# Batch 0's queries and keys loaded as rows of four tokens and turned by plain products, with a new order of work

## The chip, the cores and the metric

The kernel runs on one core of a Trainium2 chip. The metric is the device time of one execution in microseconds (us). The kernel before took 963.61 us (median of three runs, 963.43 to 965.06).

## The reference

Attention over 4 batches, 8 heads, 576 tokens and 64 columns a head, in two branches that are added, and then two MLP layers over all 2304 tokens. Cut to what matters:

```python
q_d, k_d, v_d = (t.reshape(B, H, S // 4, 4, D).mean(axis=3) for t in (q, k, v))
out_up = np.repeat(sm_attn(q_d, k_d, v_d), 4, axis=2)        # the pooled branch
mask = np.abs(pos[:, None] - pos[None, :]) < 4               # the local branch
scores = np.where(mask, scale * np.matmul(q, k.transpose(0, 1, 3, 2)), -1e9)
out_local = np.matmul(softmax(scores), v)
x = (out_up + out_local).transpose(0, 2, 1, 3).reshape(B * S, H * D)
h = x @ w_in
x = np.where(h > 0, h, np.exp(np.minimum(h, 0)) - 1) @ w_out
g = x @ w_gate
return (g / (1 + np.exp(-g)) * (x @ w_val)) @ w_o2
```

## The kernel before, in words

**Tokens and chunks.** A batch is cut into `NU` = 6 units of `U` = 96 tokens; three units (`UPC`) make a chunk of 288 tokens, so the first MLP layer runs over `NC` = 8 chunks, two for each batch. In each chunk it takes `NF1` = 16 steps: a step makes 128 hidden columns (`gemm1`, four products over the 512 input columns), applies the nonlinearity on ScalarE and VectorE, and adds their share to the four output banks (`gemm2`). In chunk 0 (`add_whole`, L929) these are plain fp32 products (L940, L945). In chunks 1 to 7 (`add_first`, L960) each operand is split into a high and a low part, and `products` (L911) multiplies three pairs of parts (L915 to L917). Tile `g` holds the high part of the hidden columns and, by a subtraction on GpSimd (L995), the low one. The second MLP layer follows and ends the run; the order in which it runs is touched by the change only through costs and due times.

**Weights.** They arrive as 64-bit words. `add_weights` (L396) loads a block of 512 KB on SyncE (L363, L368), and makes its fp32 words with two passes on ScalarE (L404, L407) and two on VectorE (L411, L413). `add_weights_away` does the same for the second layer's weights in halves, and stores them to DRAM (tiles `mid`, `wd`).

**Attention of batch 0.** `add_unit` (L616) loads 96 query rows and 112 key rows of all eight heads per unit (L494, runs of 256 B), turns each with four transpositions on TensorE (L633) into a tile for that unit, copies it out of PSUM, and sums queries and keys over four tokens (`add_sums`, L512). `add_local` (L529) does the banded scores of a unit (L541), the mask (L558), the maximum (L563), its subtraction, the exponential, the sum (L572), the weighting, a transposition on VectorE (L580), the spreading into the block-diagonal tile `bd`, and the value products (L606) into `f`. `add_pooled` (L685) does the pooled branch for a pair of heads: sums of values (`add_rows`, L696 on VectorE or L700 and L701 on GpSimd), scores (L717), maxima (L724), exponentials (L730), weighting (L740), transpositions (L758), value products (L774) into `xdT`. `add_split` (L885) adds `f` and `xdT` to `x`, the input of the first MLP layer; chunk 0 needs units 0 to 2 and all four head pairs.

**Attention of batches 1 to 3** runs beside the first MLP layer. `add_turned` (L648) loads queries and keys block by block (L662, runs of 128 B) into the tiles `qT` and `kT` of the whole batch, and VectorE transposes each block in place (L667). `add_double` does two units at a time, `add_pooled_all` (L781) the pooled branch.

**What sets the order.** All work is given to a planner (`Work`, L138) as tasks with an engine (or a choice of two), a cost in us, a due time, tiles read and written. `run` plays the engines forward by these costs, starts on each free engine the ready task that is due first, and emits it; so the costs and due times decide the order of each engine's instructions, and nothing else. The program then runs each engine in that order, with semaphores. The due times hang on a few numbers:

```python
START, STEP0, STEP, STEP2 = 48.0, 4.1, 3.45, 7.9
EAGER, URGENT, FREE, SLACK = 15.0, 14.0, 8.0, 1.0
spans = {1: (18, 25), 2: (40, 50), 3: (70, 80)}
```

`time1(s)` is the planned time of step `s`; `spans` says in which steps the attention of a batch is due.

## Time and profile before

| | |
|---|---|
| median of three runs | 963.61 us |
| the profiled execution | 962.43 us |
| its span on the core | 960.6 us |
| first product of the first MLP layer starts at | 49.22 us |
| TensorE matmul busy | 924.7 us (96%) |
| VectorE / ScalarE / GpSimd busy | 587.9 / 519.6 / 488.8 us |
| mean granted TensorE clock | 0.982 |

The busy time of TensorE counts pipelined products and is no measure of how close it is to its peak; what can be read from it is where it stands still. A time in a row counts from the start of the span. A line number is that of the kernel before; the changed kernel's lines are up to some 12 lower.

### The profile page before, as it was taken

To read this page: it belongs to the slowest core of one execution; us is meant where nothing else is said; L and a number is where in the kernel's file an instruction comes from. 1 tells how busy PE (TensorE), PEld (TensorE's weight loads), DVE (VectorE), ACT (ScalarE), POOL (GpSimd) and SP (SyncE) were. 2 spreads that over 40 slices of the span, in tenths; PEclk is the share of its full clock that TensorE was granted. 3 is DMA by queue.
4 is the path that set the end of the run, shared out by engine and by line. 5 is a ranking of instruction groups with operands and counts; after the bars stand their busy time and mean duration, and the time that the engine had idled before them with its cause. 6 is when DMAs were issued, how large, how long until landed. Compare 5 with 4: busy or idle time off the path is not lost.

```text
span 960.6 us, 20374 instructions
## 1 busy us (share of the span) xinstructions
PE 924.7 (96%) x7738; PEld 838.2 (87%) x7738; DVE 587.9 (61%) x1023; ACT 519.6 (54%) x1191; POOL 488.8 (51%) x554
## 2 busy tenths in 40 slices
PE   6799999999989999999899999999999999999998
PEld 4577788899979999999899988888888887899998
DVE  5999777988886687646115567222222225886773
ACT  3878864665744665656445564634333426444441
POOL 5322994564553433428932537998777939100000
PEclk8689999999999999999999999999999999999999
DMA  9899514945673444546432254440313269953331
GB/s 173 251 319 250 93 40 121 164 144 141 162 159 94 129 135 124 154 128 199 149 94 81 83 184 182 162 176 23 121 51 114 99 208 322 314 165 112 124 129 44
DMA packets 189730, 142.07 MB, mean 148 GB/s; under 512 B 101184, under 2 KB 170944, under 8 KB 189632
## 3 DMA queue, kind: packets, MB, share of 16 engines
q1 hardware_dynamic: 189488, 140.50, 50.0%
q8 instruction: 61, 1.00, 0.4%
q14 instruction: 37, 0.30, 0.1%
q10 hardware_dynamic: 144, 0.26, 0.1%
HBM read 96.68 MB, written 44.04 MB: 146 GB/s over the span
## 4 chain that ended last, share of the span: by engine, by line
PE 85%; DVE 5%; ACT 2%; POOL 2%; SPq 2%; DMA 2%; issue 2%; DVEq 0%; ACTq 0%; POOLq 0%
PE bank L915 25%; PE bank L917 24%; PE bank L916 24%; PE bank L940 4%; PE bank L945 3%; PE bank L606 1%; PE bank L541 1%; SPq L662 1%; PE bank L817 1%; PE bank L823 1%; PE warm L1416 0%; DVE e L988 0%; PE bank L870 0%; DMA kT<-in_k_dram 0%; DMA x2d<-o 0%
## 5 line engine op out<-in xcount | busy, mean ns | idle before, releaser
L995 POOL TENSOR_TENSOR g<-e,g 128x288 fp32r<-128x288 f32 x112 | 96.3, 861 | 150.3 <-ACT g L307 115.6
L915 PE MATMUL bank<-x,w 128*128 128x288 f32 x448 | 136.3, 304 | 10.0 <-DVE e L988 9.8
L915 PE MATMUL bank<-g,w 128*128 128x288 f32 x448 | 135.2, 302 | 0.0
L916 PE MATMUL bank<-x,w 128*128 128x288 f32 x448 | 132.9, 297 | 1.6 <-POOL x L903 1.6
L915 PE MATMUL bank<-xs,wu 128*128 128x512 f32 x336 | 132.6, 395 | 0.5 <-DVE blk L1119 0.5
L916 PE MATMUL bank<-g,w 128*128 128x288 f32 x448 | 132.1, 295 | 0.7 <-issue 0.7
L916 PE MATMUL bank<-xs,wu 128*128 128x512 f32 x336 | 132.6, 395 | 0.0
L917 PE MATMUL bank<-xs,wu 128*128 128x512 f32 x336 | 132.6, 394 | 0.0
L917 PE MATMUL bank<-x,w 128*128 128x288 f32 x448 | 132.4, 296 | 0.0
L917 PE MATMUL bank<-g,w 128*128 128x288 f32 x448 | 131.8, 294 | 0.0
L1119 DVE TENSOR_TENSOR blk<-bank,blk 128x512 f32<-128x512 f32 x72 | 49.7, 691 | 99.1 <-PE bank L917 90.7
L915 PE MATMUL bank<-os,ys 128*128 128x256 f32 x378 | 107.3, 284 | 1.5 <-DVE o L1119 1.0
L917 PE MATMUL bank<-os,ys 128*128 128x256 f32 x378 | 107.0, 283 | 0.4 <-DVE ys L1087 0.4
L916 PE MATMUL bank<-os,ys 128*128 128x256 f32 x378 | 106.9, 283 | 0.0
L988 DVE SCALAR_TENSOR_TENSOR e<-e,bank 128x288 f32<-128x288 f32 x112 | 50.1, 449 | 82.9 <-ACT e L992 76.9
L915 PEld LDWEIGHTS bank<-x,w 128*128 128x128 f32 x448 | 84.6, 189 | 14.4 <-DVE e L988 13.1
L1116 ACT COPY blk<-bank 128x512 f32<-128x512 f32 x72 | 42.2, 586 | 88.6 <-PE bank L917 87.2
L984 ACT ACTIVATE e<-bank 128x288 f32<-128x288 f32 x112 | 45.7, 410 | 80.4 <-PE bank L917 50.8
L916 PEld LDWEIGHTS bank<-x,w 128*128 128x128 f32 x448 | 85.2, 190 | 1.9 <-POOL x L903 1.8
L915 PEld LDWEIGHTS bank<-g,w 128*128 128x128 f32 x448 | 84.0, 187 | 3.2 <-issue 1.5
L917 PEld LDWEIGHTS bank<-g,w 128*128 128x128 f32 x448 | 84.5, 189 | 0.8 <-issue 0.8
L917 PEld LDWEIGHTS bank<-x,w 128*128 128x128 f32 x448 | 85.1, 190 | 0.0
(170 smaller groups left out, 2315.2 us busy)
## 6 DMA issues: line engine op xcount, KB each, us to landing
yr<-yd SPq DMA_DIRECT2D x27, 512.0 KB
yd<-blk SPq DMA_DIRECT2D x24, 512.0 KB
os<-od SPq DMA_DIRECT2D x42, 256.0 KB
u<-wd SPq DMA_DIRECT2D x40, 256.0 KB
wd<-mid SPq DMA_DIRECT2D x72, 128.0 KB
w<-in_moe_w_in_dram SPq DMA_DIRECT2D x16, 512.0 KB
w<-in_moe_w_out_dram SPq DMA_DIRECT2D x16, 512.0 KB
w<-in_moe_w_out_dram SPq DMA_DIRECT2D x24, 256.0 KB
```

The source lines that it names most:

```text
L541: nc.tensor.matmul(sc[j].t[s * QB:(s + 1) * QB, (u * NP + p) * QB:(u * NP + p + 1) * QB], q_of(p)[j * D:(j + 1) * D, a:a + QB], k_of(p)[j ...
L606: nc.tensor.matmul(pvs[u].t[j * D:(j + 1) * D, p * U:(p + 1) * U], tvs[u].t[:, (2 * p + j) * D:(2 * p + j + 1) * D], bd.t[:, u, j * NP + p ...
L915: nc.tensor.matmul(ps, sh, mh, start=first, stop=False, skip_group_check=more)
L916: nc.tensor.matmul(ps, sh, ml, start=False, stop=False, skip_group_check=more)
L917: nc.tensor.matmul(ps, sl, mh, start=False, stop=last, skip_group_check=more)
L940: nc.tensor.matmul(h.t[:, :T1], wi.t[:, i * P:(i + 1) * P].bitcast(F32), x.t[:, i, 0].bitcast(F32), start=i == 0, stop=i == NP - 1)
L945: nc.tensor.matmul(acc[0][i].t[:, :T1], wo.t[:, i * P:(i + 1) * P].bitcast(F32), ge(), start=f == 0, stop=f == NF1 - 1)
L984: nc.scalar.activation(e.t, h.t[:, :T1], AF.Relu, scale=-1.0)
L988: nc.vector.scalar_tensor_tensor(out=e.t, in0=e.t, scalar=-1.0, op0=ALU.add, in1=h.t[:, :T1], op1=ALU.max)
L995: add("pool", 0.82, due - URGENT, lambda e=e, g=g: nc.gpsimd.tensor_tensor(out=g.t[:, 1], in0=e.t, in1=g.t[:, 0], op=ALU.subtract), reads= ...
L1116: return add("act", ps_copy, when(m) - 20, lambda: nc.scalar.copy(d(i), ps.t[:, :w]), reads=[ps], writes=of(i))
L1119: return add("dve", ps_sum, when(m) - 20, lambda: nc.vector.tensor_tensor(out=d(i), in0=ps.t[:, :w], in1=d(i), op=ALU.add), reads=[ps], wr ...
```

## The change

Batch 0 is laid out like the other batches: queries and keys in `qT` and `kT` over the whole batch. `add_unit` is replaced by `add_first_batch`. It issues 16 loads (four head pairs, two halves of the batch, queries and keys) in rows of four tokens: 72 rows, for each of two heads 256 numbers in one run of 1 KB. Each load is turned by eight plain products with the identity (four tokens, two heads), which write every fourth column of a PSUM bank, and copied to `qT` or `kT`. Sums over four tokens are taken per load; key sums are for GpSimd alone. The pooled value sums of batch 0 go to GpSimd alone (`VS`). Tiles of batch 0's softmax lie in parts of weight slots, and two raw weight slots fewer are there for the loads of weights (12, not 14). All other edits are costs, due times and the constants above: batch 1's attention is due in steps 4.5 to 10.8 and not 18 to 25, loads ahead of a batch by 31.6 us and not 14, the conversion of the second layer's weights from 3.2 chunks on and not 2, and so on. Some 30 costs in calls of `add` change by a few hundredths to tenths of a us in the same way as the one of `negative` below.

```diff
-    CHANGE = 0.1
+    CHANGE = 0.15
...
-    U0, U1 = 2, 19
+    U0, U1 = 2, 21
...
-    START, STEP0, STEP, STEP2 = 48.0, 4.1, 3.45, 7.9
+    START, STEP0, STEP, STEP2 = 54.0, 4.58, 3.41, 7.9
     order = [(c, f) for c in range(NC) for f in range(NF1)]
+    VS, VC = EITHER[1:], (1.25,)
+    FIRST, VALUES, LATER, POOLED = -40.0, -30.4, 14.3, 20.4
-    EAGER, URGENT, FREE, SLACK = 15.0, 14.0, 8.0, 1.0
+    EAGER, URGENT, FREE, SLACK = 10.7, -0.6, 12.0, 0.0
...
-        add("pe", 0.8 * n, due + 2 - EAGER, scores, reads=reads, writes=[*sc, sm], slack=SLACK, kind="small", after=then)
+        add("pe", 0.8 * n, due + 2 - EAGER, scores, holds=[x for name in parts for x in parts[name]], writes=[*sc, sm],
+            slack=SLACK, kind="small", after=[*made, *then])
...
-    def add_unit(i, due, load_due, rows, late, v_due, first):
-
-        q0 = i * U
-        k0 = min(max(q0 - 8, 0), S - KU)
-        off = PAD + q0 - k0
-        tq, tk, tv = rows
-        add("sp", 0.5, load_due, lambda: load_rows("q", 0, q0, U, tq.t), writes=[tq], nbytes=U * H * D * 4 * 1.9)
-        add("sp", 0.5, load_due + 0.1, lambda: load_rows("k", 0, k0, KU, tk.t), writes=[tk], nbytes=KU * H * D * 4 * 1.9)
-        add("sp", 2.0, v_due, lambda: load_values(0, q0, tv.t), writes=[tv], nbytes=P * H * D * 4 * 3.1)
-        if i == 0:
-            sums[0] = sum_ring.new()
-        qT, kT = place("qT"), place("kT")
-        for which, t, dst, count, start, own in ((0, tq, qT, U, 0, 0), (1, tk, kT, KU, PAD, off)):
-            pt = att_bank()
-
-            def turn(t=t, count=count, pt=pt):
-                for p in range(NP):
-                    nc.tensor.transpose(pt.t[:, p * count:(p + 1) * count], t.t[:count, p * P:(p + 1) * P], ident[:count, :count])
-
-            def keep(engine, dst=dst, count=count, start=start, pt=pt):
-                copy(engine, dst.t[:, :, start:start + count], pt.t[:, :NP * count].rearrange("p (a t) -> p a t", a=NP))
-
-            add("pe", 0.4, first - EAGER, turn, reads=[t], writes=[pt, dst], slack=SLACK, kind="small")
-            add(COPIER, (0.5, 0.55), first + 1, keep, reads=[pt], writes=[dst], second=1)
-            early.append(add_sums(first + 2, lambda dst=dst, own=own: dst.t[:, :, own:own + U].rearrange("p a (g r) -> p a g r", r=R),
-                lambda which=which: sums[0].t[:, which, :, i * GU:(i + 1) * GU], [dst], [sums[0]], (0.56, 1.1)))
-        xfs = add_local(i, 1, due + late, lambda p: qT.t[:, p], lambda p: kT.t[:, p], [qT, kT], off, [tv])
-        early.extend(qT.readers + kT.readers)
-        return xfs[0]
-
-    early, summed = [], {}
+    def add_first_batch(rows, ready):
+
+        sums[0] = sum_ring.new()
+        parts = {name: [longs[name].new(lambda p=p: [p]) for p in range(NP)] for name in ("qT", "kT")}
+        made = {}
+        for k, (p, u, which) in enumerate((p, u, which) for p in range(NP) for u in range(2) for which in range(2)):
+            name, start = (("qT", 0), ("kT", PAD))[which]
+            t, dst, pt = rows[k], parts[name][p], att_bank()
+            cols = slice(start + u * UPC * U, start + (u + 1) * UPC * U)
+            add("sp", 0.5, FIRST + 0.5 * k, lambda t=t, p=p, u=u, name=name: nc.sync.dma_start(
+                out=t.t, in_=rows_of(name[0], 0, u, 2 * p, 2 * p + 2)), writes=[t], nbytes=HALF * 2048 * 1.2)
+
+            def turn(t=t, pt=pt):
+                for r in range(R):
+                    for j in range(2):
+                        nc.tensor.matmul(
+                            pt.t[j * D:(j + 1) * D, :UPC * U].rearrange("c (g r) -> c g r", r=R)[:, :, r],
+                            t.t[:, j, r * D:(r + 1) * D], ident[:HALF, :HALF], start=True, stop=True)
+
+            add("pe", 0.62, FIRST + k - EAGER, turn, reads=[t], writes=[pt, dst], slack=SLACK, kind="small", after=ready[:1])
+            made[which, p, u] = add(COPIER, (0.41, 0.45), FIRST + k + 1, lambda engine, dst=dst, pt=pt, cols=cols: copy(
+                engine, dst.t[:, cols], pt.t[:, :UPC * U]), reads=[pt], writes=[dst], second=1)
+            summed.setdefault((0, p), []).append(add_sums(
+                FIRST + k + 2, lambda dst=dst, cols=cols: dst.t[:, cols].rearrange("p (g r) -> p g r", r=R),
+                lambda which=which, p=p, u=u: sums[0].t[:, which, p, u * HALF:(u + 1) * HALF], [], [sums[0]], (0.45, 0.9)[which:],
+                holds=[dst], after=[made[which, p, u]], engines=EITHER[which:]))
+        return parts, made
+
+    summed = {}
...
-        if b == 1:
-            clear = lambda: [nc.gpsimd.memset(x.t[:, a:z], 0.0) for x in parts["kT"] for a, z in ((0, PAD), (PAD + S, LONG))]
-            after = [*after, *early, add("pool", 1.0, load_due, clear, writes=parts["kT"], after=early)]
...
-            add(EITHER, (1.0, 1.25), due, lambda engine, u=u, t=t: add_rows(u, t.t, engine), reads=[t], writes=[vs])
+            add(VS, VC, due, lambda engine="pool", u=u, t=t: add_rows(u, t.t, engine), reads=[t], writes=[vs])
...
-        if b:
-            add(EITHER, (0.78, 1.3), due + 4.3, weight, reads=[pr, su], writes=[pr])
-        else:
-            add("dve", 0.78, due + 4.3, lambda: weight("dve"), reads=[pr, su], writes=[pr])
+        add(EITHER, (0.78, 1.15), due + 4.3, weight, reads=[pr, su], writes=[pr])
...
-            add("act", 0.45, due - URGENT, negative, reads=[h], writes=[e])
+            add("act", 0.41, due - URGENT, negative, reads=[h], writes=[e])
...
-        rows = [parts(2) for _ in range(NU)]
+        rows = [x for _ in range(2 * NP) for x in parts(2)]
...
-            xfs[n] = add_unit(n, 4.0 * n, -40 + 2 * n, rows=(*rows[n], vals[n]), late=0.0 if n < UPC else 24.0,
-                v_due=-20.0 + n if n < UPC else 30.0 + n, first=0.5 * n - 8.0)
-            if n == 0:
-                load_mask()
+            late = n >= UPC
+            add("sp", 2.0, LATER + n if late else VALUES + n, lambda n=n: load_values(0, n * U, vals[n].t), writes=[vals[n]], nbytes=P * H * D * 4 * 3.1)
+            turned_by = [t for (which, p, u), t in made.items() if u == (late or 0) or (which and (n == UPC - 1 or n == UPC))]
+            xfs[n], = add_local(n, 1, 2.5 * n + 68.6 * late, parts, turned_by, [vals[n]], ready[1:], (), sms[n])
         for p in range(NP):
-            add_pooled(0, p, 16.0 + 0.5 * p, -28 + p, raws=praws[2 * p:2 * p + 2], pr=probs[p])
+            add_pooled(0, p, POOLED + 1.5 * p, -28 + p, raws=praws[2 * p:2 * p + 2], pr=probs[p], prT=turneds[p])
...
-            return time1(2 * NF1) + (time1(6.9 * NF1) - time1(2 * NF1)) * m / (2 * len(w2))
+            return time1(3.2 * NF1) + (time1(6.5 * NF1) - time1(3.2 * NF1)) * m / (2 * len(w2))
...
-        spans = {1: (18, 25), 2: (40, 50), 3: (70, 80)}
+        spans = {1: (4.5, 10.8), 2: (50.5, 52.5), 3: (76.5, 119.4)}
         split = UPC
         for b in range(1, B):
             lo, hi = (time1(s) for s in spans[b])
             after = [words["in", 10 if b == 1 else NF1 - 1]]
-            parts = add_turned(b, lo, lo - 14, after)
-            add_pooled_all(b, lo + 4, lo - 10, 3.0)
+            parts = add_turned(b, lo, lo - 31.6, after)
+            add_pooled_all(b, lo + 2.3, lo - 24.0, 7.3)
             for m in range(NU // 2):
-                due = lo + 6 + (hi - lo) * 2 * m / NU
-                xfs[b * NU + 2 * m], xfs[b * NU + 2 * m + 1] = add_double(b, m, due, due - 18, parts, after, [words["out", 10]])
+                due = lo + 5.0 + (hi - lo) * 2 * m / NU
+                xfs[b * NU + 2 * m], xfs[b * NU + 2 * m + 1] = add_double(b, m, due, due - 19.7, parts, after, [words["out", 10]])
...
-                    made += [add_split(split, xfs[split], time1(NF1 * (split // UPC)) - 12.0)]
+                    made += [add_split(split, xfs[split], time1(NF1 * (split // UPC)) - 1.4)]
```

**TensorE, batch 0's attention.** Two pieces in the middle of the prefix, first before: transpositions (L633) of a unit, local scores (L541) and pooled scores (L717) in turn.

```order
L633 MATMUL bank<-ident,w 128x96 x4
L541 MATMUL bank<-kT,qT 32x32 x32
L633 MATMUL bank<-ident,w 128x112 x4
L541 MATMUL bank<-kT,qT 32x32 x32
L717 MATMUL bank<-sums 72x144 x8
L606 MATMUL bank<-bd,w 64x96 x8
L717 MATMUL bank<-sums 72x144 x4
```

And now, from the first turning product (L630) on; L538 are the local scores of units, L710 the pooled scores, L748 the pooled transpositions, L764 the pooled value products, L605 the local ones.

```order
L630 MATMUL bank<-ident,w 64x72 x80
L710 MATMUL bank<-sums 72x144 x4
L630 MATMUL bank<-ident,w 64x72 x48
L538 MATMUL bank<-kT,qT 32x32 x96
L710 MATMUL bank<-sums 72x144 x8
L748 MATMUL bank<-ident,w 72x72 x8
L538 MATMUL bank<-kT,qT 32x32 x32
L710 MATMUL bank<-sums 72x144 x4
L605 MATMUL bank<-bd,w 64x96 x16
L764 MATMUL bank<-w,vs 64x144 x4
```

The 16 turning groups of eight stand ahead of all local scores; one pooled pair of heads is scored among them.

**VectorE, ahead of the first product of the first MLP layer.** Before: L411 and L413 make a weight's words, L893 makes `x`.

```order
L411 SCALAR_TENSOR_TENSOR bank<-bank,w 128x512
L413 SCALAR_TENSOR_TENSOR w<-w,bank 128x512
L309 COPY xdT<-bank 128x144
L411 SCALAR_TENSOR_TENSOR bank<-bank,w 128x512
L413 SCALAR_TENSOR_TENSOR w<-w,bank 128x512
L558 TENSOR_TENSOR sm<-bank,mask 128x128 x2
L572 TENSOR_REDUCE st<-sm 128x8
L573 TENSOR_SCALAR st<-st 128x8
L574 RECIPROCAL st<-st 128x8
L309 COPY xdT<-bank 128x144
L563 TENSOR_REDUCE st<-sm 128x8
L893 TENSOR_TENSOR x<-f,xdT 128x4x96 x3
```

Now L412 and L414 make the words, and L883 makes `x`.

```order
L556 TENSOR_TENSOR w<-bank,mask 128x128 x2
L561 TENSOR_REDUCE st<-w 128x8
L556 TENSOR_TENSOR w<-bank,mask 128x128 x2
L578 STREAM_TRANSPOSE w<-w 128x256
L561 TENSOR_REDUCE st<-w 128x8
L883 TENSOR_TENSOR x<-f,xdT 128x4x96 x3
L412 SCALAR_TENSOR_TENSOR bank<-bank,w 128x512
L414 SCALAR_TENSOR_TENSOR w<-w,bank 128x512
L412 SCALAR_TENSOR_TENSOR bank<-bank,w 128x512
```

The two first weights' words stood ahead of `x` and now stand behind it.

**GpSimd, ahead of chunk 2.** Before: L995 is the subtraction for `g` (one a step), L893 and L903 make `x` of later chunks, L524 and L525 sum batch 2's keys.

```order
L995 TENSOR_TENSOR g<-e,g 128x288
L856 TENSOR_TENSOR pr<-pr,su 72x576
L995 TENSOR_TENSOR g<-e,g 128x288 x4
L893 TENSOR_TENSOR f<-f,xdT 128x384
L524 TENSOR_TENSOR half<-kT 128x288
L525 TENSOR_TENSOR sums<-half 128x144
L903 TENSOR_TENSOR x<-f,x 128x4x96 x4
```

Now the same are L985, L883, L893, L523 and L524.

```order
L985 TENSOR_TENSOR g<-e,g 128x288
L790 TENSOR_TENSOR praw<-praw 72x2x128
L791 TENSOR_TENSOR vs<-praw 72x128
L883 TENSOR_TENSOR f<-f,xdT 128x384
L985 TENSOR_TENSOR g<-e,g 128x288
L883 TENSOR_TENSOR f<-f,xdT 128x384
L790 TENSOR_TENSOR praw<-praw 72x2x128
L791 TENSOR_TENSOR vs<-praw 72x128
L893 TENSOR_TENSOR x<-f,x 128x4x96
```

The first `x` piece of chunk 2 stood behind 16 of the layer's subtractions and a key sum, and now stands behind 11 of them.

## Rows read from the trace of the kernel before

**Rows 1.** TensorE in order of time, prefix: start, duration, line, operation, count, wait.

```profile
2.53 4.78 PE L1416 MATMUL warm<-bd 128*128 128x512 bf16 x12 [2.53 <-DVE bd L1414]
...
49.22 6.71 PE L940 MATMUL bank<-x,w 128*128 128x288 f32 x16 [1.88 <-DVE x L893]
```

**Rows 2.** Busy time by stretch: PE, PEld, DVE, ACT, POOL, granted clock, DMA share, GB/s.

```profile
20.00:40.00 20.00, 13.13 (x251) 10.30 (x249) 18.49 (x54) 15.07 (x55) 9.05 (x16) 0.76 0.91 272
20.00:22.00 2.00, 0.26 (x7) 0.05 (x5) 1.93 (x6) 0.54 (x1) 1.33 (x3) 1.00 0.90 220
40.00:42.00 2.00, 1.79 (x11) 1.21 (x9) 1.98 (x5) 1.91 (x6) 1.11 (x7) 0.50 1.10 340
```

**Rows 3.** SyncE's queue in order of time, prefix: issue of value and weight loads.

```profile
13.55 6.10 SPq L705 DMA_DIRECT2D w<-in_v_dram  x8
19.77 7.27 SPq L494 DMA_DIRECT2D w<-in_v_dram  x13
27.09 0.45 SPq L363 DMA_DIRECT2D w<-in_moe_w_in_dram  x1
```

**Rows 4.** ScalarE in order of time, prefix: first pass over a loaded weight.

```profile
34.59 0.68 ACT L407 ACTIVATE w<-w 128x512 int32<-128x512 uint32 x1
```

**Rows 5.** TensorE in order of time, prefix: pooled value products at both clocks.

```profile
34.75 0.72 PE L774 MATMUL bank<-prT,vs 72*64 72x144 f32 x8
...
37.96 1.23 PE L774 MATMUL bank<-prT,vs 72*64 72x144 f32 x8 [1.66 <-DVE sm L558]
```

**Rows 6.** Groups of VectorE, 0 to 50 us: busy us, mean ns, then idle before.

```profile
L724 DVE TENSOR_REDUCE mx<-bank 72x2 f32<-72x288 f32 x8 | 3.2, 441 | 0.8 <-PE bank L717 0.7
L893 DVE TENSOR_TENSOR x<-f,xdT 128x384 f32<-128x384 f32 x3 | 3.2, 1113 | 0.0
L740 DVE TENSOR_TENSOR w<-w,su 72x576 f32<-72x576 f32 x4 | 2.9, 745 | 0.0
L558 DVE TENSOR_TENSOR sm<-bank,mask 128x128 f32<-128x128 f32 x12 | 2.8, 272 | 0.0
...
L563 DVE TENSOR_REDUCE st<-sm 128x8 f32<-128x256 f32 x6 | 2.4, 400 | 0.0
...
L580 DVE STREAM_TRANSPOSE sm<-sm 128x256 f32<-128x256 f32 x5 | 2.2, 432 | 0.0
...
L309 DVE COPY prT<-bank 72x288 f32<-72x288 f32 x4 | 1.7, 446 | 0.0
L566 DVE TENSOR_TENSOR sm<-sm,st 128x256 f32<-128x256 f32 x3 | 1.4, 481 | 0.0
...
L413 DVE SCALAR_TENSOR_TENSOR w<-w,bank 128x512 int32<-128x512 int32 x2 | 1.4, 690 | 0.1
...
L309 DVE COPY f<-bank 128x384 f32<-128x384 f32 x2 | 1.1, 558 | 0.2
...
L574 DVE RECIPROCAL st<-st 128x8 f32<-128x8 f32 x5 | 1.0, 203 | 0.2
```

**Rows 7.** Groups of GpSimd, 0 to 50 us: first pass of a pooled value sum.

```profile
L700 POOL TENSOR_TENSOR w<-w 72x256 f32<-72x256 f32 x4 | 2.9, 724 | 0.0
```

**Rows 8.** TensorE's waits, 120 to 200 us, and the largest, 200 to 530 us.

```profile
PE bank L870 <- ACT f L307: 1.7, 1, 1.7
PE bank L916 <- POOL x L903: 1.6, 1, 1.6
PE bank L916 <- issue: 0.7, 1, 0.7
PE bank L823 <- POOL sums L525: 0.5, 1, 0.5
...
PE bank L915 <- DVE e L988: 9.6, 7, 3.9
```

**Rows 9.** TensorE in order of time at 265 us, within chunk 3.

```profile
269.56 0.61 PE L915 MATMUL bank<-x,w 128*128 128x288 f32 x1 [3.91 <-DVE e L988]
```

**Rows 10.** VectorE in order of time behind it: the transposition of a key block.

```profile
268.40 0.77 DVE L667 STREAM_TRANSPOSE kT<-kT 128x576 f32<-128x576 f32 x1
```

**Rows 11.** Busy time by stretch just behind that wait (columns as in rows 2).

```profile
269.50:273.00 3.50, 3.44 (x16) 3.17 (x18) 3.11 (x7) 1.29 (x4) 1.88 (x2) 0.52 0.80 207
```

More of the change, by code (lines that the diff above doesn't have):

```diff
@@ L27 @@
 U = NB * SB
-KU = 112
 CR = 64
@@ L510, in load_values, with add_sums, pool @@
                 load_rows("v", b, a, min(hi - a, QB // 2 if hi - lo < QB else QB), t, p0 + a - lo)
-    def add_sums(due, x, to, reads, writes, cost):
+    def add_sums(due, x, to, reads, writes, cost, engines=EITHER, **kw):
         half = half_ring.new()
-        def pool(engine):
+        def pool(engine=engines[0]):
             src, dst = x(), to()
@@ L525, in pool, with add_local @@
                 nc.gpsimd.tensor_tensor(out=dst, in0=h[(*cut, 0)], in1=h[(*cut, 1)], op=ALU.add)
-        return add(EITHER, cost, due, pool, reads=reads, writes=[*writes, half])
-    def add_local(i, n, due, q_of, k_of, reads, off, tvs, then=()):
-        start = i * U if n > 1 else 0
+        return add(engines, cost, due, pool, reads=reads, writes=[*writes, half], **kw)
+    def add_local(i, n, due, parts, made, tvs, masks=(), then=(), sm=None):
         sc, pvs = [att_bank(), att_bank()], [att_bank() for _ in range(n)]
@@ L537, in scores @@
                     for s in range(NB):
[L538 to L539 removed]
+                        a = (i + u) * U + s * SB
                         for j in range(2):
@@ L599, in add_local @@
         else:
-            add("act", 2.1, due + 6, lambda: spread("act"), reads=[sm], writes=[bd])
+            add("act", 2.05, due + 6, lambda: spread("act"), reads=[sm], writes=[bd])
         def values(us):
@@ L689, in add_pooled @@
         vs = vs_ring.new()
-        mx, nm, su, prT = (small[n].new() for n in ("mx", "nm", "su", "prT"))
-        pr = pr or small["pr"].new()
+        mx, nm, su = (small[n].new() for n in ("mx", "nm", "su"))
         qk = sums[b]
@@ L718, in scores @@
                         sc[j].t[:HALF, u * G:(u + 1) * G], t[:, 0, p, u * HALF:(u + 1) * HALF], t[:, 1, p], start=True, stop=True)
-        add("pe", 0.6, due + 1 - EAGER, scores, reads=[qk], writes=[*sc, mx, nm, su, pr], slack=SLACK, kind="small")
+        add("pe", 0.6, due + 1 - EAGER, scores, holds=[qk], after=summed[b, p], writes=[*sc, mx, nm, su, pr], slack=SLACK, kind="small")
         def maxima():
@@ L1001, in gemm2 @@
                     products(acc[c][i].t[:, :T1], (wo.t[:, 0, cs], wo.t[:, 1, cs]), (g.t[:, 0], g.t[:, 1]), f == 0, f == NF1 - 1)
-            last[c] = [add("pe", 12 * 0.134, due + STEP, gemm2, reads=[wo, g], writes=acc[c], after=last.get(c, ()), slack=1.0)]
+            last[c] = [add("pe", 12 * 0.1325, due + STEP, gemm2, reads=[wo, g], writes=acc[c], after=last.get(c, ()), slack=1.0)]
             if f == NF1 - 1:
```

87 lines of the change are left out of this document (46 added, 41 removed).

## The prediction, made before the result was known

> **What bounds the kernel now.** I first read TensorE's order of time and its waits, because an engine that is busy for nearly the whole span leaves time only where it stands still. The warm-up products end at 7.31 us and the first product of the first MLP layer starts at 49.22 us, after a wait for VectorE's `x` [rows 1]. Between these two lies the attention of batch 0. From there on TensorE is the bound: the later rows show it waiting only here and there. So the run divides into three: the time to that first product (call it T0, 49.2 us here), a body of TensorE work, and the holes in the body. In the prefix VectorE is the fullest engine, 18.49 of 20 us in the stretch from 20 to 40 us [rows 2]. Chunk 0's products, and those after it, read the same tiles in both kernels, so I take the body as unchanged and ask for T0 and for the holes. All sums are made against the profiled execution, 962.43 us (span 960.6); the median of the runs shown is 1.2 us above it.
>
> **The loads, part by part.** The 12 loads of queries and keys (2.5 MB, in runs of 256 B) become 16 loads of 72 rows of 1 KB pieces (16 x 144 KB, 2.36 MB). The same form of load exists already: the eight value loads of the pooled branch, under way from 20 to 22 us, where the core moved 220 GB/s [rows 2]. At that rate 2.36 MB take 10.7 us, one load every 0.67 us. They are first in the queue now, so all should be there at about 14 us. I cost them at nothing: the turning products, below, take them at the same pace and don't begin before 7.31 us. If that cover were gone (turning in half the time), the last load would set the pace, and nothing is gained below 14 us.
>
> Behind them the values of units 0 to 2 (13 transfers, 7.27 us of issue), the pooled values (8, 6.10 us), the values of units 3 to 5 (13 again) and only then the first weights [rows 3]. Before, nine weight loads stood ahead of the last 13. By these prices the weights are issued at about 12 + 7.3 + 6.1 + 7.3 = 32.7 us. The first one was issued at 27.09 us and read by ScalarE at 34.59 us [rows 3, 4], at most 7.5 us on; so it is usable by 40.2 us, and VectorE asks for it at 43 us. Cover: some 3 us. If it is gone, every us of lateness is a us of T0.
>
> **Turning.** The 24 transpositions of `add_unit` go, 16 groups of eight products with the identity come. No row shows that form. The nearest is the pooled value product: 72 rows, 64 columns out, four products of 144 columns, as many columns as eight of 72. It took 0.72 us (0.65 to the next start) at 34.75 us and 1.23 us at 37.96 us [rows 5], the two levels of the clock, 2.4 and 1.2 GHz. At 0.65, with one pooled score group (taken at the same 0.65) between them, turning ends at 7.31 + 17 x 0.65 = 18.4 us. At 1.23 from about 10 us on, 12 groups cost 0.58 more each, 7.0 us in all. I take the low price, since nothing interrupts the row of products once it has begun, and keep the other for the range and a rival. There is a row against my choice: between 40 and 42 us TensorE was busy 1.79 of 2 us, largely with this form, and the granted clock was 0.50 [rows 2].
>
> The Trainium skill ("TensorE: Matmul & The Clock Gate", Part 1) says the throttled clock is the default state and that sustained activity releases it. By that rule the unbroken row of turning products runs at full clock and my low price stands; by the row just named it would not, and T0 would be 7 us later.
>
> **VectorE up to `x`.** The first batch of local scores (0.8 us) ends at 19.2 us. From there VectorE's new list up to the three `x` additions holds, at the means of [rows 6]: 12 mask additions, 3.3; 10 maxima and sums of weights (6 and 4), 4.0; 4 transpositions, 1.7; 6 pooled maxima, 2.6; 2 pooled weightings, 1.5; 2 softmax products, 1.0; 2 copies to `f`, 1.1; 2 to `prT`, 0.9; and 17 short scalar operations at 0.20, 3.4. That is 19.5 us, and 21.2 us at the 92% that VectorE reached before. It would stand at 40.4 us. The three `x` additions follow as before, 3.2 us: 43.6 us. New is that the first weight's words, two passes of 0.69 us, stand behind them and not before: 45.0 us. So T0 = 45.0, a gain of **4.2 us**. Without any idle time it would be 43.3; with turning at the low clock, 52.
>
> What left VectorE is work on other engines. GpSimd now takes all eight pooled value sums, two passes of at most 0.72 us each [rows 7], 11.6 us, between its key sums and `x`; ScalarE takes the spreading of weights. Both had room in the prefix (9.05 and 15.07 of 20 us [rows 2]), so I cost them at nothing. If GpSimd falls behind, the fourth pooled value product is late and `x` with it.
>
> **The holes after T0.** From 120 to 200 us four waits make 4.5 us [rows 8]: on ScalarE's `f`, on GpSimd's `x` for chunk 2, on an unnamed cause and on GpSimd's sums. All belong to batch 1, whose work then runs up to the start of chunk 2. The new order starts it in chunk 0 (planned steps 4.5 to 10.8, not 18 to 25), and GpSimd's first `x` pieces for chunk 2 now stand behind the 11th to 13th `g` subtraction, not all behind the 16th. I take these **4.5 us** as gone. The holes from 200 us on, the largest being 3.9 us at 265 us [rows 9], I leave. There a key transposition started only at 268.40 us, as its load landed, with the `e` that TensorE needed behind it on VectorE [rows 10]. The tasks of load and transposition for batches 1 to 3 are the same functions, with the same assumed slack, so the same can happen again; the conversions of later weights, spread out anew, neither add nor take work. The changed costs and due times act through the order alone.
>
> Sum: 962.43 - 4.2 - 4.5 = 953.7, and as the profiled run is just below the median, **954 us**.
>
> **The rivals.**
> - *The low clock in the prefix.* Turning costs 7.0 more: 953.7 + 7.0 = 960.7 us. For it speaks the granted clock of 0.50 at 40 us; against it, that the turning products stand in one row from 7.31 us. Chance 0.15.
> - *Slower: transpositions queue behind their loads in each of batches 1 to 3.* One such block costs 3.9 us [rows 9], and in the stretch behind it the clock was 0.52 for 3.5 us [rows 11], some 1.7 us more: 5.6 us. Three new ones make 16.8: 970.5 us. It decides from the second on, since one is less than the 8.7 us of gain and two are 11.2. For it: the loads of a batch still wait until the last scores of the batch before have left the same tiles. Against: they are planned 31.6 us ahead of their use, not 14. Chance 0.17.
> - *The prefix gets no shorter*: GpSimd's 11.6 us, the pooled chain or late weights hold `x` until 49 us. Then only the holes go: 957.9 us, or 962 if they don't either. Chance 0.13.
> - *The later holes go too.* Those from 200 to 530 us, 9.6 us behind VectorE's `e` [rows 8], end with the new order: 944 us. Chance 0.12.
>
> **How the numbers follow.** My forecast, 949 to 960 us by itself, has 0.43. The range 943 to 966 leaves out most of the slower rival and a little below. A measurement of this kernel can tell 0.2%, 1.9 us, from no change. Faster than 961.7 us: forecast 0.43, later holes 0.12, half of the low clock 0.08, most of the unshortened prefix 0.10, together 0.73. Within it: the other half of the low clock and the rest of the prefix, 0.10. Slower: 0.17.
>
> **What would show it.** Right: the first product of the layer at 44 to 46 us; turning groups 0.65 us apart at a granted clock of 1.00 until about 18 us; VectorE fed without gaps from 19 us; no TensorE wait above 0.5 us between 120 and 200 us. Wrong: turning groups 1.2 us apart; the first product at 49 us or later, then with GpSimd's value sums or a weight load as what it waited for; waits of several us behind `e` with a transposition of `qT` or `kT` just ahead of it on VectorE. If T0 is as forecast and the total is not, the holes in chunks 1 to 7 are where I erred.

## The result, and the profile of the changed kernel

The change takes **953.75 us** (median of 4 runs, 950.18 to 954.69) where before takes 964.34 us (four runs, one more than above, 963.43 to 965.16): a ratio of 0.9884, 95% interval 0.9856 to 0.9912. The forecast was 954. The sum came out, but not by its terms. The profiled execution takes 953.54 us (span 951.7, before 960.6), and this is where the 8.9 us of span came from:

| stretch | before | change | difference | forecast |
|---|---|---|---|---|
| T0, first product of the layer | 49.2 | 53.0 | +3.8 | -4.2 |
| from T0 to chunk 1's first split product (at 111.9, 115.5) | 62.7 | 62.5 | -0.2 | 0 |
| from there to the end | 848.7 | 836.2 | -12.5 | -4.5 |

The prefix got longer, and the gain behind it is nearly three times the forecast one. (Some 0.7 us of the last row is no gain: batch 1's first pooled scores, eight products of L813, now stand in chunk 0.) The first fence is TensorE in order of time in the changed kernel (start, duration, line, operation, count, wait); it answers to [rows 1]. L630 are the turning products (16 records to a group), L538 local scores, L710 pooled scores, L605 local values, L764 pooled values, L930 the layer's first product.

```profile
7.76 1.72 PE L630 MATMUL bank<-ident,w 72*64 72x72 f32 x48
10.32 6.29 PE L630 MATMUL bank<-ident,w 72*64 72x72 f32 x112 [0.84 <-ACT qT L306]
16.54 1.24 PE L710 MATMUL bank<-sums 64*72 64x144 f32 x8
17.71 6.03 PE L630 MATMUL bank<-ident,w 72*64 72x72 f32 x96
23.66 2.21 PE L538 MATMUL bank<-kT,qT 64*32 64x32 f32 x192
...
28.43 1.72 PE L710 MATMUL bank<-sums 64*72 64x144 f32 x12 [1.87 <-issue]
...
47.44 0.71 PE L764 MATMUL bank<-w,vs 72*64 72x144 f32 x6 [0.18 <-POOL vs L694]
51.53 1.55 PE L605 MATMUL bank<-bd,w 128*64 128x96 f32 x16 [3.38 <-ACT bd L306]
53.00 5.36 PE L930 MATMUL bank<-x,w 128*128 128x288 f32 x16
```

The first three groups take 1.72 us, the last six 6.03, 1.0 us each: turning ends at 23.7 us, not at 18.4. The windows tell why (stretch, length, TensorE's busy time, granted clock, DMA share, GB/s): the clock falls within the stretch from 11 to 12 us, while TensorE is busy all of it. The last row has all engines, in the columns of [rows 2]: VectorE is no longer full (14.14 of 20 us, before 18.49), it waits.

```profile
8.00:10.00 2.00, 1.48 (x48) 1.00 0.75 173
10.00:11.00 1.00, 0.68 (x21) 1.00 0.62 171
11.00:12.00 1.00, 1.00 (x26) 0.56 0.69 219
12.00:14.00 2.00, 2.00 (x40) 0.50 0.74 199
14.00:20.00 6.00, 6.00 (x90) 0.50 0.34 83
20.00:40.00 20.00, 14.84 (x382) 12.49 (x380) 14.14 (x44) 10.88 (x47) 12.14 (x24) 0.50 0.58 124
```

What happens behind turning: GpSimd's list has its local work ahead of the pooled value sums, and waits there for VectorE (GpSimd in order of time). Its eight value sums (L693, L694) run from 34.19 to 47.38 us; the last pooled value product, `x` and the weight's words follow one upon the other.

```profile
33.04 0.61 POOL L575 TENSOR_TENSOR w<-w,st 128x256 f32<-128x256 f32 x1 [3.33 <-DVE st L572]
...
34.19 0.72 POOL L693 TENSOR_TENSOR w<-w 72x256 f32<-72x256 f32 x1
...
46.93 0.45 POOL L694 TENSOR_TENSOR vs<-w 72x128 f32<-72x128 f32 x1
```

VectorE at the end of that chain, the three `x` additions and the first weight's two passes:

```profile
48.66 1.90 DVE L883 TENSOR_TENSOR x<-f,xdT 128x384 f32<-128x384 f32 x3
50.48 0.69 DVE L412 SCALAR_TENSOR_TENSOR bank<-bank,w 128x512 int32<-128x512 int32 x1
51.20 0.69 DVE L414 SCALAR_TENSOR_TENSOR w<-w,bank 128x512 int32<-128x512 int32 x1
```

So the weight is whole at 51.89 us, and TensorE adds 1.1 us to that: the value product of unit 3, which chunk 0 does not need, stands ahead of the layer and waits for ScalarE's spreading until 51.53. SP's queue (answering to [rows 3]) issues the first weight at 38.03 us, not at 32.7.

```profile
22.88 3.47 SPq L698 DMA_DIRECT2D w<-in_v_dram  x8
26.39 11.59 SPq L493 DMA_DIRECT2D w<-in_v_dram  x13
38.03 0.53 SPq L364 DMA_DIRECT2D w<-in_moe_w_in_dram  x1
```

ScalarE's first pass over it, answering to [rows 4], comes at 46.33 us:

```profile
46.33 0.67 ACT L408 ACTIVATE w<-w 128x512 int32<-128x512 uint32 x1
```

Behind chunk 0, the waits of [rows 8] are nearly gone. TensorE's waits (us in total, times, longest), first from 120 to 200 us, then from 200 to 530:

```profile
PE bank L905 <- DVE e L978: 1.2, 2, 0.6
PE bank L860 <- DVE sm L556: 0.4, 1, 0.4
...
PE bank L905 <- DVE e L978: 1.3, 2, 0.8
PE bank L906 <- POOL g L985: 0.7, 2, 0.5
```

All waits listed for these stretches sum to 2.2 and 2.0 us; before they summed to 4.8 and 10.2. That is 10.8 of the 12.5 us; by the prediction's estimate 1.7 us more stood in the slow clock behind the wait of 3.9 us [rows 9, 11].

### The profile page after: what moved, and what is told of

It is laid out like the page before. It is cut to its first block, busy times and chain, and to the rows that moved or that the text cites. A ratio compares the mean times of both kernels' runs of the same rounds, so it can differ in the third digit from the quotient of the medians.

```text
span 951.7 us, 20820 instructions
## 1 busy us (share of the span) xinstructions
PE 928.6 (98%) x7946; PEld 841.8 (88%) x7946; DVE 585.7 (62%) x1027; ACT 512.4 (54%) x1178; POOL 498.7 (52%) x572
## 4 chain that ended last, share of the span: by engine, by line
PE 81%; POOL 7%; DVE 3%; issue 3%; DMA 3%; ACT 2%; SPq 0%; POOLq 0%; DVEq 0%; ACTq 0%
PE bank L905 23%; PE bank L907 23%; PE bank L906 23%; PE bank L930 3%; PE bank L935 3%; POOL w L452 2%; DMA w<-in_moe_w_gate_dram 2%; PE bank L630 1%; PE bank L605 1%; POOL g L985 1%; PE bank L538 1%; PE bank L813 1%; POOL wu L1077 1%; PE bank L807 1%; POOL oh L1077 1%
## 5 line engine op out<-in xcount | busy, mean ns | idle before, releaser
L985 POOL TENSOR_TENSOR g<-e,g 128x288 fp32r<-128x288 f32 x112 | 98.0, 876 | 136.2 <-ACT g L306 87.2
L905 PEld LDWEIGHTS bank<-x,w 128*128 128x128 f32 x448 | 84.0, 188 | 5.5 <-DVE e L978 3.8
L905 PEld LDWEIGHTS bank<-g,w 128*128 128x128 f32 x448 | 84.0, 187 | 2.8 <-issue 1.7
L906 PEld LDWEIGHTS bank<-g,w 128*128 128x128 f32 x448 | 84.6, 189 | 1.3 <-POOL g L985 1.1
L906 PEld LDWEIGHTS bank<-x,w 128*128 128x128 f32 x448 | 84.7, 189 | 0.1
L907 PEld LDWEIGHTS bank<-g,w 128*128 128x128 f32 x448 | 84.5, 189 | 0.0
```

Source lines behind the costliest of these rows:

```text
L905: nc.tensor.matmul(ps, sh, mh, start=first, stop=False, skip_group_check=more)
L906: nc.tensor.matmul(ps, sh, ml, start=False, stop=False, skip_group_check=more)
L907: nc.tensor.matmul(ps, sl, mh, start=False, stop=last, skip_group_check=more)
L985: add("pool", 0.86, due - URGENT, lambda e=e, g=g: nc.gpsimd.tensor_tensor(out=g.t[:, 1], in0=e.t, in1=g.t[:, 0], op=ALU.subtract), reads= ...
```

## The experiments

Two questions: what made the gain behind chunk 0, and why the prefix is late. For the first, theory A says the order (due times, spans, leads, costs), theory B the new layout of batch 0, which no longer stands in the way of batch 1. Each run is compared with before on the same chip. "Behind" is the span less the start of chunk 1's first split product.

**New layout, old numbers.** All numbers of the planner but those of batch 0's new parts are set back:

```diff
-    START, STEP0, STEP, STEP2 = 54.0, 4.58, 3.41, 7.9
+    START, STEP0, STEP, STEP2 = 48.0, 4.1, 3.45, 7.9
...
-    EAGER, URGENT, FREE, SLACK = 10.7, -0.6, 12.0, 0.0
+    EAGER, URGENT, FREE, SLACK = 15.0, 14.0, 8.0, 1.0
...
-        spans = {1: (4.5, 10.8), 2: (50.5, 52.5), 3: (76.5, 119.4)}
+        spans = {1: (18, 25), 2: (40, 50), 3: (70, 80)}
...
```

> The new layout of batch 0 with the order numbers of before for all else (START, STEP0, EAGER, URGENT, FREE, SLACK, the costs, spans, load leads). Theory A, by which the gain is made by the order in chunks 1 to 7 and the new prefix loses some 4 us: the first product of the layer again at 51 to 55 us, the TensorE waits between 120 and 530 us back at 10 to 15 us, so the time at 963 to 969 us. Theory B, by which the holes closed because batch 0 no longer stands in the way of batch 1's loads and tiles: the waits stay at about 4 us and the time within 950 to 957 us.

Measured: 972.13 us (6 runs), ratio 1.0071 (1.0046 to 1.0095): slower than before. T0 is 54.5 us, chunk 1 begins at 118.7, behind 851.4 us. From 200 to 530 us the waits are back:

```profile
PE bank L905 <- DVE e L978: 12.4, 10, 2.7
```

As theory A has it, and 3 us worse than it expected. With the old numbers the new layout gains nothing.

**Old layout, new numbers.** The reverse, in the kernel before. SLACK stays 1.0 (with the change's 0.0 the old layout gave no program), so this is the reverse in all numbers but one.

> The old layout of batch 0 with the order numbers of the change (all but SLACK, which stays 1.0). Theory A (the order closes the holes after 120 us, whatever the layout): the first product at 47 to 52 us, the TensorE waits between 120 and 530 us at 4 to 7 us, the time at 948 to 954 us. Theory B (the layout closes them): waits of 10 us and more there, the time at 958 us or above.

Measured: 958.87 us (4 runs), ratio 0.9940 (0.9920 to 0.9961). T0 49.1, behind 840.2 us. The waits are 5.1 us from 120 to 200 and 4.1 from 200 to 530. So neither theory alone: the numbers bring 8.5 of the 12.5 us behind chunk 0 on the old layout too; the last 4 stayed away (a local value product waits 3.3 us at 142 us), and whether that is due to the old layout or to the SLACK of 1.0, this run cannot tell. In front the numbers cost 2.1 us (chunk 1 at 114.0 us, before 111.9), part of which is batch 1's work moved there.

**One number of them: the spans.**

```diff
-        spans = {1: (4.5, 10.8), 2: (50.5, 52.5), 3: (76.5, 119.4)}
+        spans = {1: (18, 25), 2: (40, 50), 3: (70, 80)}
```

> The change with the spans of before for batches 1 to 3: (18, 25), (40, 50), (70, 80). Theory: starting batch 1 in chunk 0 (step 4.5) and spreading batch 3 (76.5 to 119.4) is what closed the holes, those from 120 to 200 us above all: waits of 4 us and more return there, the time is 956 to 962 us. Rival: the waits stay as in the change and the time at 950 to 955 us.

Measured: 959.42 us (3 runs), ratio 0.9971 (0.9947 to 0.9995), behind 846.8 us. Setting back the three spans alone costs 10.6 us there, of the 15.2 that all old numbers cost on this layout (851.4 against 836.2). Listed waits make 5.6 of the 10.6, and 0.7 is the pooled scores, which stand behind chunk 0 again; the rest was not traced. The theory's place was wrong: from 120 to 200 us the waits are 3.2 us (2.2 in the change; 4 and more were expected), from 200 to 530 us 6.6 (2.0 in the change), most of them behind `e` again:

```profile
PE bank L905 <- DVE e L978: 4.8, 5, 2.5
PE bank L905 <- DVE o L308: 1.0, 1, 1.0
PE bank L905 <- ACT o L306: 0.8, 1, 0.8
```

Which of the three spans does it was not tried.

**Another: the lead of the loads of batches 1 to 3.**

```diff
-            parts = add_turned(b, lo, lo - 31.6, after)
+            parts = add_turned(b, lo, lo - 14, after)
```

> The change with one number of before: the loads of queries and keys of batches 1 to 3 planned 14 us, not 31.6 us, ahead of their transpositions. Theory: this lead is what closed the holes behind VectorE's e after 200 us (a transposition that waits for its load with an e behind it). Then waits of 2 to 4 us behind e return where batches 2 and 3 begin, 4 to 8 us in all, and the time is 957 to 961 us. Rival: the lead alone does little, since the spans and the urgency of e set the order: waits behind e stay under 4 us in all and the time at 950 to 955 us.

Measured: 950.03 us (2 runs), ratio 0.9860 (0.9840 to 0.9880), behind 835.5 us. The lead does nothing that two runs can show, though in before a late key load stood behind the largest hole [rows 10].

**The prefix: the clock.** Two full-array products ahead of each turning group, which compute nothing that is used:

```diff
             def turn(t=t, pt=pt):
+                nc.tensor.matmul(pt.t[:, :256], ident.bitcast(BF16)[:, :P], ident.bitcast(BF16), start=True, stop=True)
+                nc.tensor.matmul(pt.t[:, :256], ident.bitcast(BF16)[:, :P], ident.bitcast(BF16), start=True, stop=True)
                 for r in range(R):
```

> The change with two full-array bf16 products of 256 columns ahead of each group of turning products, which add work only. If the clock is what made a group take 0.96 us, and such products hold it: the granted clock stays at 1.00 to the end of turning, a group takes 0.8 us with its two, turning ends at 21.5 us in place of 23.7, and the first product of the layer comes at 50 to 51 us: time about 951.5 us. If loads or copies set the pace of the groups, turning ends at 23.5 to 24 us again and nothing changes: 953 to 954 us. If the clock falls all the same, a group takes 1.2 to 1.4 us, turning ends at 27 to 29 us and the time is 956 to 959 us.

Measured: 954.51 us (4 runs), ratio 0.9897 (0.9856 to 0.9938). The clock held throughout turning (columns as in the windows above):

```profile
8.00:24.00 16.00, 16.00 (x296) 1.00 0.52 129
```

But a group with its two took 0.975 us from start to start, not 0.8:

```profile
8.78 0.28 PE L628 MATMUL bank<-ident 128*128 128x256 bf16 x1
8.89 0.27 PE L629 MATMUL bank<-ident 128*128 128x256 bf16 x1
9.10 0.72 PE L632 MATMUL bank<-ident,w 72*64 72x72 f32 x16
9.75 0.28 PE L628 MATMUL bank<-ident 128*128 128x256 bf16 x1
```

From the first product of the two to the second it takes 0.11 us, from there to the group 0.21, and the group 0.65, where it takes 0.53 in an unbroken row: the change of shape seems to cost too. Turning ended at 24.05 us, where the expectation's second branch had it, but with TensorE busy for all 16 us there is no wait for loads or copies. T0 came at 54.3. So a miss on the price; and that the two products kept the clock up is not shown by one execution, since it also held in some without them (below). T0 again lies 29 to 31 us behind the end of turning (29.3 in the change, 30.3 here), and behind is 835.5 us, as in the change (836.2).

**The start of the layer.** Unit 3's value product behind the first step, and 24 products of 256 columns ahead of that step; the order of all else is unchanged.

```diff
...
-            begun.append(1)
+            begun.append(1); [nc.tensor.matmul(h.t[:, :256], ident.bitcast(BF16)[:, :P], ident.bitcast(BF16), start=True, stop=True) for _ in range(24 if f == 0 else 0)]
             for i in range(NP):
                 nc.tensor.matmul(
                     h.t[:, :T1], wi.t[:, i * P:(i + 1) * P].bitcast(F32), x.t[:, i, 0].bitcast(F32), start=i == 0, stop=i == NP - 1)
-
+            [fn() for fn in put_off[:1] * (f == 0)]
```

> The change with the value product of unit 3 moved behind the first step's products of the layer, and 24 full-array bf16 products of 256 columns ahead of that step, in TensorE's idle time. If that value product's wait on ScalarE's spreading (3.4 us) holds the layer back only by what lies behind the weight's words, the first product comes at 51.9 to 52.2 us in place of 53.0; if the 24 keep the clock up, the first two steps take 4.2 us in place of 5.4. Together 2.2 us: 951.5 us. If the wait were the whole cause, it would come at 49.6 us and the time be 949 us. If the words of the weight are the bound and the clock falls all the same: 953 to 954 us.

Measured: 949.54 us (4 runs), ratio 0.9842 (0.9816 to 0.9867); expected 951.5. The profiled execution (span 945.7) says more than the edits do. Before either of them acts, its clock stayed at 1.00 to 20 us; turning ended at 17.8 us, and T0 came 8 us earlier (VectorE, then TensorE):

```profile
41.70 1.90 DVE L883 TENSOR_TENSOR x<-f,xdT 128x384 f32<-128x384 f32 x3
...
44.99 1.24 PE L930 MATMUL bank<-x,w 128*128 128x288 f32 x4 [1.07 <-DVE w L414]
```

All engines from 19.2 to 41.7 us, up to `x`, in the columns of [rows 2]:

```profile
19.20:41.70 22.50, 16.60 (x425) 13.38 (x419) 18.01 (x57) 14.27 (x52) 19.05 (x33) 0.77 0.71 175
```

**The change once more.** Is the clock in turning a matter of the execution?

> The changed kernel itself once more, unaltered. Theory C: whether the clock falls during turning differs from execution to execution, and with it the first product of the layer comes at about 45 or at about 53 us; of those 8 us some 3.5 to 6 reach the end. Then the executions spread over 949 to 955 us, those at a mean clock near 0.99 below 951.5 and those near 0.98 above 953. Theory D: the clock falls at 11 to 12 us in all executions of this kernel, and what differed in the kernel with the moved value product was due to its edits: then all executions lie at 953 to 955 us at a mean clock of 0.98.

Measured: 951.72 us (5 runs, 947.28 to 953.1), ratio 0.9860 (0.9837 to 0.9883). Theory C holds for the clock: the same kernel, now at 1.00 up to 20 us, ends turning at 18.0 us.

```profile
9.90 3.72 PE L630 MATMUL bank<-ident,w 72*64 72x72 f32 x112 [0.84 <-ACT qT L306]
...
14.84 3.22 PE L630 MATMUL bank<-ident,w 72*64 72x72 f32 x96
...
47.47 1.55 PE L605 MATMUL bank<-bd,w 128*64 128x96 f32 x16 [5.74 <-ACT bd L306]
```

TensorE's window from 14 to 20 us, which had a clock of 0.50 above:

```profile
14.00:20.00 6.00, 5.80 (x298) 1.00 0.27 62
```

It does not hold for what comes of it. T0 is 48.95 us, since now the weight is late: ScalarE stood 3.92 us until the load issued at 37.75 us had landed at 43.54. And chunk 1 begins at 116.2 us, no earlier than in the first execution of the change (115.5, with T0 at 53.0). TensorE lost it between 92 and 102 us: 2.7 us of waits for `g`, with the clock at 0.50 behind the longer one, and ScalarE waiting for the last weights from 85 to 95 us (1.48, 1.12 and 0.97 us). The span, 951.3 us, is the same. The clock of a whole execution does not sort the times well either (0.990 at 952.3 us, 0.983 at 951.7).

**What makes the clock fall?** TensorE waits 0.84 us after the third group for ScalarE's table load (1.28 us at 8.57 us). One tiny copy ahead of the loads takes it away:

```diff
-        nc.vector.memset(turned["bd"], 0.0)
+        nc.vector.memset(turned["bd"], 0.0); nc.scalar.copy(turned["bd"][:, 1, 0, :8], turned["bd"][:, 1, 0, 8:16])
```

> The change with one tiny copy on ScalarE before the first load lands, so that its table load (1.28 us, at 8.57 us) no longer stands between the third and the fourth group of turning products. If the 0.84 us in which TensorE waits there are what lets the clock fall in turning: the granted clock stays at 1.00 until turning ends at 17 to 18 us, the first product comes at 44 to 45.5 us, and all executions lie at 948 to 951 us. If the clock falls there in any case in some executions: spread as before, 949 to 955 us, at best 0.8 us less.

Measured: 950.5 us (4 runs, 949.8 to 954.9), ratio 0.9868 (0.9844 to 0.9892). The gap went and another came: the pooled scores after the tenth group waited 2.85 us for GpSimd's sums, the clock was at 0.50 from 16 us, T0 53.3. Inconclusive.

**All edits so far**, and the clears of two value tiles moved from GpSimd (at 15.29 and 36.70 us, with SP's value loads behind them) to VectorE's idle start.

> Four edits together: the early table load, the value product of unit 3 behind the first step, 24 full-array bf16 products ahead of the first step, and the two clears of value tiles (0.52 us each) taken from GpSimd's list to VectorE's idle start, so that the value loads and the weights behind them no longer wait for GpSimd. If the first weights' lateness is what holds the layer's first steps in the kernel with the moved value product (waits of 1.1, 0.6 and 0.8 us): weights issued 3 to 6 us earlier, these waits gone, the time 944.5 to 947.5 us. If ScalarE's list or the pooled chain holds them: the first product at 44 to 45 us again and 947 to 950 us.

Measured: 950.73 us (6 runs, 946.8 to 953.9), ratio 0.9858 (0.9833 to 0.9883). The clock fell again behind a wait of 1.3 us for the sums; T0 51.0. Neither branch of the expectation; with the clock low the weights were in time, and no wait stood between 60 and 110 us.

**The mask's copies and clears** also go from GpSimd to VectorE, so that the key sums no longer wait for its load:

```diff
-                nc.gpsimd.tensor_copy(mask[:, e], mask[:, 0])
+                nc.vector.tensor_copy(mask[:, e], mask[:, 0])
...
```

> The four edits of the earlier run with all of them, and the mask's copies and clears moved from GpSimd's list to VectorE's, so that GpSimd's key sums no longer wait for the mask's load (to 11.5 us) and TensorE's first pooled scores, between the 10th and the 11th turning group, no longer wait 1.3 us for those sums. Theory E: the clock falls in turning where TensorE has a gap there (0.84 us for the table load, 1.3 to 2.8 us for the sums). With both gaps gone it stays at 1.00 until turning ends at 17 us; the first product comes at 44 to 45.5 us, all executions lie at 945 to 948 us, clocks at 0.99 or above. If the clock falls without a gap, executions spread over 946 to 954 us as they did.

Measured: 948.67 us (4 runs, 946.7 to 949.6), ratio 0.9843 (0.9829 to 0.9858): with T0 at 43.2 us and a span of 944.8 the shortest prefix and the lowest median, 3 and 5 us under the two medians of the change. By the ratio, the fair comparison across chips, it is level with the run with the altered start (0.9842), and its interval still overlaps those of both runs of the change. All four executions have a mean clock of 0.993 to 0.995. The time is a little above the expectation (945 to 948 us): chunk 1 begins at 109.4 us, 66.2 us behind T0 and not 62.5, with 2.1 us of waiting for `g` at 91 us. With GpSimd's clears out of its way, SP issues the first weight here at 32.92 us, which is the forecast's 32.7:

```profile
32.92 1.02 SPq L364 DMA_DIRECT2D w<-in_moe_w_in_dram  x1
```

**Fillers in the later gaps** of the prefix (14 and 40 products in two places).

> The run with the mask moved, and 14 full-array bf16 products of 224 columns inside the second pooled score group and 40 of 128 columns ahead of the first value product, where TensorE stood for 2.1 and 2.7 us with the clock falling to 0.50 behind it. If these keep the clock up: 1.00 from 4 to 50 us, pooled scores of 1.9 us at 1.0, the first product at 42 to 44 us and 943.5 to 946.5 us. If VectorE, ScalarE and GpSimd set the pace there: the first product at 44 to 45 us and no gain over the run without them.

Measured: 954.44 us (4 runs), ratio 0.9904 (0.9887 to 0.9920). A miss, and it refutes theory E as it stands: up to the 16th group both kernels issue the same on TensorE, but here the clock fell to 0.54 between 16 and 18 us, with gaps of 0.2 us only, where the run above kept 1.00 behind a gap of 0.43. TensorE at the last two groups here, and its window (columns as above):

```profile
16.12 2.19 PE L630 MATMUL bank<-ident,w 72*64 72x72 f32 x32 [0.22 <-DMA w<-in_q_dram]
...
16.00:18.00 2.00, 1.88 (x32) 0.54 0.51 95
```

And in the run above:

```profile
16.02 1.22 PE L630 MATMUL bank<-ident,w 72*64 72x72 f32 x32 [0.43 <-DMA w<-in_q_dram]
...
16.00:18.00 2.00, 1.98 (x127) 1.00 0.38 80
```

Behind that, the fillers stood on the path itself (the 40 took 3.66 us, the 24 ahead of the layer 4.72), and T0 was 54.3. Executions at a mean clock of 0.992 and 0.993 took 953.4 and 955.2 us, so it is not the clock alone that makes this version slow.

**Weights ahead of the late values**, to see whether their arrival is a floor for chunk 0: on SP six weight loads pass the value transfers of units 3 to 5.

> The run with the mask moved, and on SP six weight loads put ahead of the 13 value transfers of units 3 to 5. Theory F: the arrival of the 32 weights is a second floor for chunk 0, whatever the time of the first product (ScalarE waited for weight loads at 83 to 90 us and TensorE 2.1 us for g there). Weights issued from 24 us, not 33 us: the first product at 41 to 42.5 us, no TensorE wait on g at 85 to 95 us, the first split product of chunk 1 at 104 to 107 us in place of 109.4, and 943 to 946.5 us. If the memory is as busy either way, or the value product of unit 3 now waits for its late values and blocks the layer: the first split product at 109 us or later and 947 to 950 us.

Measured: 950.39 us (5 runs, 947.3 to 952.0), ratio 0.9837 (0.9820 to 0.9853). A miss: the late value transfers now occupied SP from 30.0 to 44.1 us, the seventh weight came behind them, T0 was 45.2 and the wait for `g` at 93 us still 1.8 us. That the memory brings the same in the same time either way, as the expectation's second branch supposes, fits this but was not measured; behind was 839.0 us (835.4 in the run with the mask moved), mostly for small waits on other lines.

## Why the prediction was right, and where it was wrong

**The total** was right by luck: two errors of opposite sign, T0 8 us later than forecast, and behind chunk 0 8 us better. By its own signs the prediction was wrong in the prefix (the first product at 49 us or later) and nearly right from 120 to 200 us (longest wait 0.6 us; it asked for 0.5).

**Turning, the step that failed first:** "I take the low price, since nothing interrupts the row of products once it has begun". It is interrupted: by a table load after the third group, and in some executions by the pooled scores after the tenth. But the gaps do not decide it: the clock fell behind gaps of 0.2 us in the run with the fillers, and held behind 0.43 in the run with the mask moved. Both prices were about a fifth too high: at 1.00 a group takes 0.53 us (3.72 us for seven; forecast 0.65), at 0.50 about 1.0 (forecast 1.23). Which of them is paid differs between executions of the same kernel. In the profiled one turning ends 5.3 us later than forecast (23.7, not 18.4); the other 2.7 us of T0 arise behind it. Of eleven profiled executions with the new layout and no fillers among the turning products, the clock held through turning in six and fell within it in five; T0 came at 43.2 to 49.0 us in the six and at 51.0 to 54.5 us in the five. The rival with the low clock, at 0.15, gave T0 = 52; it was 53.0. By these eleven its chance was near a half.

The Trainium skill ("TensorE: Matmul & The Clock Gate", Part 1) says that the chip watches TensorE's activity in windows that do not begin anew with a kernel, so that the point of a change varies from run to run. That the point varies agrees with these traces (the fall within 11 to 12 us in the change, at about 16 us in the run with the fillers); that the same kernel falls in one execution and holds through all of turning in another goes beyond it. Its rule that sustained activity releases the clock, weighed in the prediction, is not borne out by the turning products: the clock fell in a stretch where TensorE was busy 1.00 of 1.00 us.

**The list up to `x`** met its forecast in one execution, and there too not by its terms. With the start of the layer altered and the clock at 1.00 through turning, `x` was whole at 43.60 us (forecast 43.6) and the first product came at 44.99 (forecast 45.0). But VectorE was not fed without gaps: it was busy 18.0 of 22.5 us (80%), where the sum had 19.5 of 21.2 (92%), so a shorter list and longer waits made up for each other. GpSimd, costed at nothing for its room, was the fuller engine, with 19.05 of 22.5 us, and the last pooled value product waited 0.47 us for its sums. In the second run of the unaltered change the clock held as well, and T0 was 48.95, not 45.0. A fall in turning shifts the whole chain, through VectorE's masks, GpSimd's local subtraction and the value sums behind it on the same list.

**The loads:** the 16 loads cost nothing, as forecast, apart from gaps of 0.2 to 0.4 us at the last groups in two of the later runs. The first weight at 32.7 us was wrong by 5.3: the step costed SP's transfers, and not what they wait for on another engine. GpSimd clears two value tiles in the order of its list, and SP stood from 12.16 to 15.84 us and within the 11.59 us of the late values; with the clears moved away the weight was issued at 32.92. Hidden behind the low clock, it is the next late thing when the clock holds: in the second run of the change ScalarE stood 3.92 us for the weight, with the last copy to `xdT`, and so `x`, behind it on its list. Unit 3's value product ahead of the layer was overlooked; behind the weight's last words it cost 1.1 us (51.89 to 53.00), and 1.7 in the second run (47.23 to 48.95).

**T0 is not worth its full length.** The sum took the body as unchanged. With T0 at 43 to 49 us and batch 1 begun in chunk 0, that chunk needs 64.6 to 67.3 us, not 62.5. TensorE then waits 1.4 to 2.7 us for `g` at about 90 us, and where unit 3's value product was moved behind the first step, it takes some 1.5 us of chunk 0 too. In the kernel with the altered start 8 us of T0 brought 4.8 (chunk 1 at 110.7 us, not 115.5). That the weights' arrival holds it at `g` is read from ScalarE's waits; the last run did not prove it. The run with the old spans had T0 at 48.1 us, neither that wait nor ScalarE's, and 62.7 us for chunk 0: so batch 1's work and loads in that chunk seem to be part of the floor (the weights were issued earlier there too, the first at 34.0 us, so the two are not told apart).

**The holes, the step that failed second:** "The holes from 200 us on ... I leave." It argued that the tasks and their slack are the same functions, and that changed costs and due times act through the order alone. They do, and the order is the point: all waits listed there went from 10.2 to 2.0 us. The rival "the later holes go too", at 0.12, is what happened behind chunk 0. From 120 to 200 us the forecast 4.5 us were 2.6 (4.8 to 2.2). The passage saw one cause, a transposition that waits for its load; the planned lead of those loads, set back alone, cost nothing that two runs show, and the spans are most of it. Which of them, and by which of the tasks they move, is open. The slower rival did not come: in the profiled execution no wait of TensorE from 120 to 530 us reached 0.9 us.

## What to carry to other kernels

Where a step has a price at each level of TensorE's clock, treat both prices as outcomes that the same kernel may show, even where its products stand in one unbroken row; and profile a kernel more than once before its prefix is explained. When a change moves the due times of later work, take one number at a time and time it: here the lead that looked like the cause was worth nothing that two runs could show, and three planned spans were worth some 10 us behind chunk 0. Count what a queue waits for on other engines (the clear of a tile ahead of its load), and ask what is late next before a shorter prefix is booked in full.

## What the runs showed of the hardware that was not expected

The same program had TensorE's clock at 1.00 until 20 us in one execution and at 0.50 from 12 us in another, with the same gap of 0.84 us ahead of it. In eleven executions no length of gap sorts those that fell from those that held: gaps of 0.22 us went with a fall, and 0.84 and 0.57 us without one. With two full-array bf16 products of 256 columns to each group it held throughout in the one execution profiled, which is no more than six executions without them did. What decides is open.
